# Queries and state of a recurrent attention moved into 64-row halves by DMA; x kept in w_in's row order; no state after the last group

## The chip, the cores and the metric

The kernel runs on 1 core of one Trainium2 chip. The metric is the device time of one launch in microseconds (us). Three runs of the kernel before took 397.42, 398.54 and 398.75 us; their median is 398.54 us.

## What is computed

Two blocks are joined. The first is a gated linear recurrence with a state per head, the second a feed-forward layer with a SoLU activation and a layer norm. The reference, cut to what matters:

```python
# q, k, v, alpha: (B=4, H=8, S=768, D=48)
state = np.zeros((B, H, D, D))
for t in range(S):
    state = alpha[:, :, t, :, None] * state + np.einsum('bhd,bhe->bhde', k[:, :, t], v[:, :, t])
    y[:, :, t] = np.einsum('bhd,bhde->bhe', q[:, :, t], state)
x = y.transpose(0, 2, 1, 3).reshape(B * S, H * D)      # 3072 x 384
h = x @ w_in                                           # 384 x 1024
e = np.exp(h - h.max(-1, keepdims=True))
solu = h * e / (e.sum(-1, keepdims=True) + 1e-09)
ln = (solu - mean(solu)) / np.sqrt(var(solu) + 1e-06) * g_ln
out = ln @ w_out                                       # 1024 x 384
```

The weights w_in and w_out arrive as 64-bit floats; the kernel reads both 32-bit words and makes f32 values of them.

## The kernel before, in words

The function that runs is `fast_path`. The 768 time steps are cut into 6 groups (G) of 128 (P). A group holds all 4 batches and all 8 heads, so 512 tokens (T4). Within a group the recurrence is turned into matrix products: scores of queries against keys under a triangular mask, the product of the masked scores with the values, and a read of the state that came in from the groups before. `scan_back` and `scan_on` are DVE scans that make the running products of alpha.

*Layout of a head.* A head has 48 rows (D). They are split into its first 32 (E0) and its last 16 (E1). Partitions hold four quarters of 32, one per batch. Blocks 0 to 7 hold the first 32 rows of the heads, blocks 8 to 11 the last 16 rows of two heads each. So `qv` has 16 blocks: 8 of first rows, and 8 in which the last rows of one head stand and those of its neighbour are zero (`apart` at L237 makes them from `qe` with `parity`). The state has the same 16 blocks, and `vn` holds the values with 80 columns (VW) per head, the last 16 dimensions at column 48.

*State read.* `read_state(n)` for n = 0 to 3 gives PE 32 matmuls each, through `y_mm` (L300): a tile of 32 rows by 32 columns at row 32b (batch) and column 32r. `read_values` adds the product of `vn` with the masked scores `sT` to the same PSUM banks (64 matmuls of 128 rows by 32 columns), and ACT copies them out as x (L331). `keys_back` (L287, L289) turns the keys round again, and `next_state` (L342, L349, L351) multiplies them with the values and adds to the state: 48 matmuls into two banks. `decay` (L251, L254) multiplies the state on POOL by the product of a whole group's alphas.

*Order of x.* The rows of x stand in blocks of 32 first dimensions of the heads, and then the last 16 of pairs of heads. To fit, `fetch` brings w_in's rows in this order: 16 copies of 32 or 16 rows for each call (L542).

*Feed-forward.* `up_mm` (L366) and `up_act` (L380 to L382) make h, e and the products; `down` (L477) multiplies with w_out, and `finish` (L495 to L511) scales and stores. `bits` (L572 to L584) makes f32 weights of the 64-bit ones on DVE, and `in_range` (L559, L560) tests their range on ACT.

*What sets the order.* It is written out by hand (`manual_schedule`); every engine works through its instructions in the order in which the program lists them. A first stretch handles group 0 and group 1's preparation. Then comes the loop over g = 1 to 5 with 8 steps s each. A step issues `up(g, s)`, half a `down` of the group before, and pieces of the attention of group g+1, which a table places in front (`head`), behind, in the middle or at the tail of the step:

```python
head={4: "keys_back", 5: "masked0", 6: "masked1"},
behind={0: "v keys", 1: "on2 on0 on1", 2: "lasts firsts", 3: "apart", 5: "decay", 6: "alpha", 7: "back"},
tail={4: "scores0", 5: "scores1", 6: "begin read0 read1", 7: "values"},
middle={7: "read2 read3"},
```

`masked` (L279) multiplies scores with the mask on DVE, `queries` (L244) and `keys` (L233) multiply with the alpha products on POOL, `firsts` and `lasts` (L184, L187) are DVE transposes. SP issues nearly all DMAs, in program order: loads of alpha, q, k (L132, L144), of v (L170; for group 0 L178, followed by POOL copies at L180), of weights (L542), and the stores (L511). In the compiled program each of these DMAs also waits for the eighth before it.

Of the kernel before, what the change touches and what calls it, by code (L numbers as in the profile page):

```python
# [9 lines left out]
FP = mybir.dt.float32  # L10
# [22 lines left out]
def fast_path(ctx, tc, q, k, v, alpha, moe_w_in, moe_w_out, moe_g_ln, out):  # L33
# [31 lines left out]
    const = pool("const", 1)  # L65
    two = pool("two", 4)
    ring = pool("ring", 3)
# [37 lines left out]

    VW = 80
    vn = const.tile([P, B, H, VW], FP, name="vn")
    state = const.tile([P, 2 * H, VW], FP, name="state")
    last = [slice(48, 80), slice(32, 64)]
    SW = P + 1  # L110
# [10 lines left out]
    kT = const.tile([P, NB, P], FP, name="kT")  # L121
    kg = const.tile([P, NB, P], FP, name="kg")
    sT = const.tile([P, B, H, P], FP, name="sT")
# [25 lines left out]
    def ends_of(src, tag=None):  # L149

        ends = ring.tile([P, T4], FP, name=tag) if tag else two.tile([P, T4], FP, tag="two", name="ends")
        ends = ends.rearrange("p (b d) -> p b d", b=B)
        nc.scalar.copy(out=ends.rearrange("p b (h d) -> p b h d", h=H), in_=by_token(src)[:, :, :, E0:D])
        return ends

    def turned(src, ends, out, blocks=range(NB)):

        x = by_token(src)
        for j in blocks:
            for b in range(B):  # L160
# [4 lines left out]
                )  # L165

    def load_v(g):
        t = slice(g * P, (g + 1) * P)
        for dst, src in ((slice(0, E0), slice(0, E0)), (slice(48, 64), slice(E0, D))):
            nc.sync.dma_start(  # L170
                out=vn[:, :, :, dst].rearrange("p b h d -> p (b h) d"),
                in_=v[:, :, t, src].rearrange("b h p d -> p (b h) d"),
            )

    def load_v_first(slot):
        x = slots[slot].rearrange("p (n d) -> p n d", d=D)
        y = vn.rearrange("p b h d -> p (b h) d")
        nc.sync.dma_start(out=x, in_=v[:, :, 0:P].rearrange("b h p d -> p (b h) d"))  # L178
        for dst, src in ((slice(0, E0), slice(0, E0)), (slice(48, 64), slice(E0, D))):
            nc.gpsimd.tensor_copy(out=y[:, :, dst], in_=x[:, :, src])  # L180


# [48 lines left out]
    def keys(g):  # L231
        for part in (slice(0, H), slice(H, NB)):
            nc.gpsimd.tensor_tensor(out=kT[:, part], in0=kT[:, part], in1=hk[:, part], op=ALU.mult)  # L233

    def apart():
        for i in range(2):
            nc.scalar.mul(  # L237
                out=qv[:, H : 2 * H].rearrange("p (j i) t -> p j i t", i=2)[:, :, i], in_=qe, mul=parity[:, i : i + 1]
            )
# [6 lines left out]
    def decay(g):  # L246

        if g == 0:
            return
        s = state[:, 0:H, 0:64]  # L250
        nc.gpsimd.tensor_tensor(out=s, in0=s, in1=h4[:, 0:H, 1:2].to_broadcast([P, H, 64]), op=ALU.mult)  # L251
        for i in range(2):
            s = state[:, H : 2 * H, 0:64].rearrange("p (j i) e -> p j i e", i=2)[:, :, i]
            nc.gpsimd.tensor_tensor(out=s, in0=s, in1=h4[:, H:NB, 1:2].to_broadcast([P, NP, 64]), op=ALU.mult)  # L254

# [28 lines left out]
    def keys_back(g, t=None):  # L284
        t = t or banks("tp", [NP, P], 3)
        for j in range(NB):
            nc.tensor.transpose(out=t[j // NP][:, j % NP], in_=kT[:, j], identity=ident)  # L287
        for i in range(3):
            nc.scalar.copy(out=kg[:, NP * i : NP * i + NP], in_=t[i])  # L289

    parts = [(a, [(NP * a + r, slice(0, E0)) for r in range(NP)]) for a in range(2)]
    parts += [(2, [(2 * r + i, last[i]) for r in range(NP)]) for i in range(2)]
    reading = {}

    def y_mm(b, a, r, row, lhsT, rhs, stop=False):
        begun = reading["begun"]
        nc.tensor.matmul(  # L300
            y_bank(b)[quarter(r), a], lhsT=lhsT, rhs=rhs, start=(b, r) not in begun, stop=stop,
            tile_position=(row, 32 * r), skip_group_check=True,
        )
        begun.add((b, r))
# [9 lines left out]

    def read_state(n):
        a, hs = parts[n]
        for rows in (0, H):
            for r, (h, e) in enumerate(hs):
                for b in range(B):
                    p = quarter(b)  # L320
                    y_mm(b, a, r, 32 * b, state[p, rows + h, e], qv[p, rows + h])

    def read_values(g, batches=range(B)):
        if 0 in batches:
            gr[g]["x"] = pair.tile([P, KC, B, P], FP, name="x")
        for b in batches:
            for n, (a, hs) in enumerate(parts):
                for r, (h, e) in enumerate(hs):
                    y_mm(b, a, r, 0, vn[:, b, h, e], sT[:, b, h], n == len(parts) - 1)
        for b in batches:  # L330
            nc.scalar.copy(out=gr[g]["x"][:, :, b], in_=reading["y"][b])  # L331

    def next_state(g):
        kv = banks("kv", [H, 64], 2)
        for j in range(NB):
            for b in range(B):
                if j < H:
                    o, e = kv[0][quarter(b), j], vn[:, b, j, 0:64]
                else:
                    i = 2 * (j - H)  # L340
                    o, e = kv[1][quarter(b), i : i + 2], vn[:, b, i : i + 2, 0:64]
                nc.tensor.matmul(  # L342
                    o, lhsT=kg[:, j, quarter(b)], rhs=e, start=True, stop=True, tile_position=(0, 32 * b),
                    skip_group_check=True,
                )
        for i in range(2):
            s = state[:, H * i : H * i + H, 0:64]
            if g == 0:
                nc.scalar.copy(out=s, in_=kv[i])  # L349
            else:  # L350
                nc.vector.tensor_tensor(out=s, in0=s, in1=kv[i], op=ALU.add)  # L351

# [30 lines left out]
    def running(g, f):  # L385

        d = gr[g]
        if f == 1:
            d["p"] = one.tile([P, 2, T4], FP, name="p")
            if g == G - 1:  # L390
                d["pu"] = two.tile([P, T4], FP, tag="two", name="pu")
        if g == G - 1:
# [54 lines left out]
    def last_norm():  # L447
# [4 lines left out]
        for b in range(B):  # L452
            for r in range(4):
# [4 lines left out]
                )  # L458
        tt = two.tile([P, B, 32], FP, tag="two", name="cols_u")
        nc.vector.transpose(out=tt.rearrange("p b t -> p (b t)"), in_=t.rearrange("p b t -> p (b t)"))  # L460
# [68 lines left out]
    def fetch(i, slot, n=1):  # L529
# [6 lines left out]
        else:  # L536
            rows = moe_w_in[:, f * P : f * P + w].rearrange("(h d) f -> h d f", d=D)
            parts = [(slice(E0 * r, E0 * r + E0), c, rows[NP * c + r, 0:E0]) for c in range(2) for r in range(NP)]
            parts += [(slice(E1 * h, E1 * h + E1), 2, rows[h, E0:D]) for h in range(H)]
        for rows, c, src in parts:  # L540
# [21 lines left out]
    def bits(i, part=None):  # L562
# [3 lines left out]
        if part != 1:  # L566
            made[i] = [
                two.tile([P, F], FP, tag="two", name=x).rearrange("p (c f) -> p c f", c=hi.shape[1])
                for x in ("top", "low")
            ]  # L570
# [66 lines left out]
    nc.gpsimd.memset(state, 0.0)  # L637
    load_v_first(0)
    fetch(0, 3, 2)
# [12 lines left out]
    t = three("tp_a", [(ps_a, "a0"), (ps_a, "a1"), (ps_a, "a2")])  # L652
    turned(an, ends_of(an), t)
    for i in range(3):
        nc.scalar.copy(out=aT[:, NP * i : NP * i + NP, 1:SW], in_=t[i])  # L655
        scan_back(0, i)
    t = three("tp_k", [(ps_a, "a3"), (ps_h, "h"), (ps_h, "h")])
    turned(kn, ends_of(kn), t)
    alpha_over(0)
# [5 lines left out]
    t = three("tp_q", [(ps_o, "o"), (ps_o, "o"), (ps_a, "a0")])  # L665
    turned(qn, ends_of(qn), t)
    for i in (2, 0, 1):
# [82 lines left out]
    nc.vector.tensor_tensor(out=qe, in0=tq[2], in1=aT[:, H:NB, 1:SW], op=ALU.mult)  # L750
    apart()
    finish(0)
    decay(1)
    in_range(7)
    for i in range(2):
        scan_on(1, i)
        part = slice(NP * i, NP * i + NP)
        nc.vector.tensor_tensor(out=qv[:, part], in0=tq[i], in1=aT[:, part, 1:SW], op=ALU.mult)  # L758
    down(2, 0)
    scores(1, 0)  # L760
# [10 lines left out]
    read_begin()  # L771
    read_state(0)
    read_state(1)
    down(3, 1)
    read_state(2)
    read_state(3)
    alpha_over(2)
    load(alpha, an, 3)
    for i in range(3):
# [3 lines left out]
    load(k, kn, 3)  # L783
    scan_on(2, 2)
    scan_on(2, 0)
    read_values(1)
# [7 lines left out]
        behind={0: "v keys", 1: "on2 on0 on1", 2: "lasts firsts", 3: "apart", 5: "decay", 6: "alpha", 7: "back"},  # L794
        tail={4: "scores0", 5: "scores1", 6: "begin read0 read1", 7: "values"},
        middle={7: "read2 read3"},
    )
    first = dict(
        head={3: "keys_back", 5: "masked0", 6: "masked1"},
        behind={0: "v", 1: "on1", 2: "lasts firsts", 3: "apart", 5: "decay", 7: "alpha back"},  # L800
        tail={4: "scores0", 5: "scores1", 6: "begin read0 read1", 7: "values"},
        middle={7: "read2 read3"},
    )

    def attend(a, what):
# [9 lines left out]
        elif what[:2] == "on":  # L815
            scan_on(a, int(what[2]))
        elif what == "lasts":
            lasts(qn, qe)
# [7 lines left out]
        elif what == "apart":  # L826
            apart()
        elif what == "decay":
            decay(a)
        elif what == "keys_back":  # L830
            keys_back(a)
        elif what[:6] == "scores":
# [15 lines left out]
        elif what == "values":  # L848
            read_values(a)
            next_state(a)  # L850

# [530 lines left out]
```

## Time and profile before

| | |
|---|---|
| span of the profiled execution | 399.0 us |
| time of the runs, median (range) | 398.54 us (397.42 to 398.75) |
| PE busy | 378.3 us, 95%, 4929 records |
| weight loads (PEld) busy | 229.1 us, 57% |
| DVE / ACT / POOL busy | 254.3 / 145.9 / 115.6 us |
| up and down projections on PE (L366, L477) | 135.5 and 133.6 us |
| state read (L300, qv and state) | 1280 records, mean 278 ns |
| next state (L342) | 576 records |
| keys back (L287) | 72 records |
| mean granted PE clock | 0.985 |

How to read it: PE is the matmul engine, PEld its weight loads, which run beside it. A group of instructions is named by line, engine, operation and `out<-in`, with the tile's shape (rows*columns) for PE. A 32-bit matmul leaves two records. Many small matmuls run at once on different parts of the array, so the busy times of single records overlap, and the cost of a stage is read from the timeline: the start of what follows minus its own start. In the timeline a row is the start in us, the length in us, engine, line, operation, and the number of records merged; brackets hold the idle time before it and what ended it. A window's row names the busy time of every engine, the granted clock, the share of the DMA engines and GB/s.

### The profile page before, as it was taken

To read this page: it belongs to the slowest core of one execution; us is meant where nothing else is said; L and a number is where in the kernel's file an instruction comes from. 1 tells how busy PE (TensorE), PEld (TensorE's weight loads), DVE (VectorE), ACT (ScalarE), POOL (GpSimd) and SP (SyncE) were. 2 spreads that over 40 slices of the span, in tenths; PEclk is the share of its full clock that TensorE was granted. 3 is DMA by queue.
4 is the path that set the end of the run, shared out by engine and by line. 5 is a ranking of instruction groups with operands and counts; after the bars stand their busy time and mean duration, and the time that the engine had idled before them with its cause. 6 is when DMAs were issued, how large, how long until landed. Compare 5 with 4: busy or idle time off the path is not lost. (4 is left out here: it accounts for less than half of the span.)

```text
span 399.0 us, 11125 instructions
## 1 busy us (share of the span) xinstructions
PE 378.3 (95%) x4929; PEld 229.1 (57%) x4929; DVE 254.3 (64%) x415; ACT 145.9 (37%) x253; POOL 115.6 (29%) x118
## 2 busy tenths in 40 slices
PE   8686999987989999999999999999999999999995
PEld 8673435555665457555557555666556575555552
DVE  1977878996897858795574884665864413444510
ACT  2634657644314415224253143342152132223200
POOL 5010000021031993438130456210475110333200
PEclk9996999998999999999999999999999999999999
DMA  9967958511366302913040931004200000000011
GB/s 184 196 165 174 224 185 160 134 28 60 81 161 99 81 3 65 161 45 92 2 102 26 155 89 32 14 11 74 28 20 21 23 3 21 20 21 18 24 41 48
DMA packets 86409, 30.82 MB, mean 77 GB/s; under 512 B 67912, under 2 KB 84560, under 8 KB 86352
## 3 DMA queue, kind: packets, MB, share of 16 engines
q1 hardware_dynamic: 85328, 29.11, 34.0%
q8 instruction: 40, 0.66, 0.7%
q10 hardware_dynamic: 1024, 0.92, 0.7%
q14 instruction: 17, 0.14, 0.1%
HBM read 25.30 MB, written 4.72 MB: 75 GB/s over the span
## 5 line engine op out<-in xcount | busy, mean ns | idle before, releaser
L366 PE MATMUL h<-x,w_in 128*128 128x512 f32 x288 | 135.5, 610 | 4.1 <-ACT sq L559 3.6
L477 PE MATMUL o<-w_out,room 128*128 128x385 f32 x384 | 133.6, 492 | 1.1 <-DVE least L223 1.1
L477 PEld LDWEIGHTS o<-w_out,room 128*128 128x128 f32 x384 | 71.8, 191 | 57.3 <-issue 16.3
L366 PEld LDWEIGHTS h<-x,w_in 128*128 128x128 f32 x288 | 53.2, 192 | 64.2 <-issue 50.7
L381 DVE TENSOR_TENSOR room<-h,e 128x512 f32<-128x512 f32 x40 | 27.5, 688 | 61.7 <-ACT e L380 61.7
L508 POOL TENSOR_TENSOR r<-sums,mhalf 128x1 f32<-128x1 f32 x20 | 12.1, 607 | 169.2 <-DVE sums L500 169.2
L380 ACT ACTIVATE e<-h 128x512 f32<-128x512 f32 x40 | 23.8, 596 | 91.9 <-PE h L366 91.9
L397 POOL TENSOR_TENSOR p<-p,e 128x512 f32<-128x512 f32 x30 | 40.9, 1365 | 24.7 <-ACT e L380 24.4
L382 ACT ACTIVATE u<-room 128x512 f32<-128x512 f32 x40 | 25.2, 631 | 42.2 <-DVE room L381 42.2
L279 DVE TENSOR_TENSOR sT<-a,mask 128x512 f32<-128x512 f32 x44 | 27.3, 683 | 16.1 <-PE a L268 16.1
L268 PE MATMUL a<-qv,kT 32*128 32x128 f32 x704 | 26.0, 286 | 4.7 <-DVE qv L758 2.0
L397 DVE TENSOR_TENSOR p<-p,u 128x512 f32<-128x512 f32 x30 | 24.7, 822 | 8.7 <-ACT u L382 8.7
L268 PEld LDWEIGHTS a<-qv,kT 32*128 32x128 f32 x704 | 22.9, 193 | 11.9 <-issue 3.3
L209 DVE TENSOR_TENSOR_SCAN hT<-aT,unit 128x516 f32<-128x516 f32 x18 | 22.2, 1282 | 8.2 <-ACT aT L655 8.1
L209 DVE TENSOR_TENSOR_SCAN aT<-aT,seed 128x516 f32<-128x516 f32 x18 | 25.7, 1428 | 0.6
L300 PE MATMUL y<-sT,vn 128*32 128x128 f32 x768 | 22.8, 274 | 1.4 <-issue 0.9
L300 PEld LDWEIGHTS y<-sT,vn 128*32 128x32 f32 x768 | 20.8, 110 | 4.0 <-issue 2.5
L233 POOL TENSOR_TENSOR kT<-kT,hT 128x1024 f32<-128x1024 f32 (+1 forms) x8 | 13.3, 1685 | 30.9 <-DVE kT L184 30.9
L331 ACT COPY x<-y 128x384 f32<-128x384 f32 x24 | 11.2, 480 | 26.4 <-PE y L300 26.4
L300 PEld LDWEIGHTS y<-qv,state 32*32 32x32 f32 x1280 | 15.3, 103 | 7.6 <-issue 4.1
L300 PE MATMUL y<-qv,state 32*32 32x128 f32 x1280 | 19.0, 278 | 0.0
L201 ACT ACTIVATE sq<-an,mone 128x1536 uint8<-128x1536 f32 x12 | 18.8, 1571 | 0.2
(140 smaller groups left out, 372.7 us busy)
## 6 DMA issues: line engine op xcount, KB each, us to landing
an<-in_alpha_dram SPq DMA_DIRECT2D x20, 192.0 KB, 4.1
out_dram<-o_sb SPq DMA_DIRECT2D x20, 192.0 KB, 1.9
room<-in_moe_w_out_dram SPq DMA_DIRECT2D x8, 384.0 KB, 3.9
kn<-in_k_dram SPq DMA_DIRECT2D x16, 192.0 KB, 3.9
qn<-in_q_dram SPq DMA_DIRECT2D x16, 192.0 KB, 3.5
vn<-in_v_dram SPq DMA_DIRECT2D x5, 512.0 KB, 5.4
room<-in_moe_w_in_dram SPq DMA_DIRECT2D x16, 128.0 KB, 3.8
kn<-in_k_dram SPq DMA_DIRECT2D x4, 384.0 KB, 5.7
```

Of the source, the lines that this page charges most:

```text
L201: nc.scalar.activation(out=sq, in_=x, func=AF.Relu, scale=sign, bias=mone, accum_out=over[:, g, i : i + 1])
L209: nc.vector.tensor_tensor_scan(out=o, data0=a, data1=s, initial=1.0, op0=ALU.mult, op1=ALU.add)
L233: nc.gpsimd.tensor_tensor(out=kT[:, part], in0=kT[:, part], in1=hk[:, part], op=ALU.mult)
L268: nc.tensor.matmul(a[b][:, i], lhsT=kT[quarter(b), kb], rhs=qv[quarter(b), qb], start=kb == h, stop=kb != h, tile_position=(32 * b, 0), sk ...
L279: nc.vector.tensor_tensor(out=sT[:, b, half * NP : half * NP + NP], in0=a[b], in1=mask[:, None, :].to_broadcast([P, NP, P]), op=ALU.mult,)
L300: nc.tensor.matmul(y_bank(b)[quarter(r), a], lhsT=lhsT, rhs=rhs, start=(b, r) not in begun, stop=stop, tile_position=(row, 32 * r), skip_g ...
L366: nc.tensor.matmul(h, lhsT=w_in[:, a, f * P : (f + 1) * P], rhs=d["x"][:, a].rearrange("p b t -> p (b t)"), start=(a == 0), stop=(a == KC ...
L380: nc.scalar.activation(out=e, in_=h, func=AF.Exp)
L381: nc.vector.tensor_tensor(out=u, in0=h, in1=e, op=ALU.mult)
L382: nc.scalar.activation(out=u2, in_=u, func=AF.Square)
L397: eng.tensor_tensor(out=p, in0=d[0][i] if f == 1 else p, in1=d[f][i], op=ALU.add)
L477: nc.tensor.matmul(d["o"][:, 0 : DM + 1], lhsT=u_of(g, f)[:, b * P : b * P + P], rhs=w_out[:, f], start=(f == 0), stop=(f == FC - 1), skip ...
```

## The change

It has three parts that go together. First, the state, the values and the keys turned round get 64 columns per head, 48 of them used, and the state stands in two halves of 64 partitions, 48 used: batch b is in half b // 2, in column block b % 2. The queries are made as before, in quarters of 32 rows; `move_q` then copies them by DMA into `q64` in the new layout, 12 copies a group: per batch the first rows of all heads, and two copies of last rows. `move_decay` does the same for the decays. A state read is then one matmul of 48 rows per head and output block where there were two of 32 rows. Second, x stands in w_in's own row order: an output block of 32 columns that crosses two heads is made by two matmuls into the same place (`last`), with zeros beside the values. `fetch` brings w_in in copies of 128 rows. Third, the last group no longer turns its keys round and makes no state. The pool `two` is replaced by four fixed slots in `lot`, three of which `q64` takes over later; v comes in one copy per batch, for group 0 too, without POOL copies.

```diff
-    VW = 80
-    vn = const.tile([P, B, H, VW], FP, name="vn")
-    state = const.tile([P, 2 * H, VW], FP, name="state")
-    last = [slice(48, 80), slice(32, 64)]
+    HW = 64
+    VW = H * HW + E1
+    vn = const.tile([P, B, VW], FP, name="vn")
+    state = const.tile([P, 2, VW], FP, name="state")
+    lot = const.tile([P, 4 * 768], FP, name="lot")
+    lots = [lot[:, 768 * i : 768 * i + 768] for i in range(4)]
+    q64 = lot[:, 0 : 2 * H * P].rearrange("p (c h t) -> p c h t", c=2, h=H)
+    dec64 = const.tile([P, 2, H], FP, name="dec64")
...
-    kg = const.tile([P, NB, P], FP, name="kg")
+    kg = const.tile([P, B, H, HW], FP, name="kg")
...
+    def held(x, n):
+        return x[:, n, 0 : H * HW].rearrange("p (h e) -> p h e", e=HW)[:, :, E1:HW]
...
-        for dst, src in ((slice(0, E0), slice(0, E0)), (slice(48, 64), slice(E0, D))):
-            nc.sync.dma_start(
-                out=vn[:, :, :, dst].rearrange("p b h d -> p (b h) d"),
-                in_=v[:, :, t, src].rearrange("b h p d -> p (b h) d"),
-            )
+        for b in range(B):
+            nc.sync.dma_start(out=held(vn, b), in_=v[b, :, t, :].rearrange("h p d -> p h d"))
...
+    def moved(dst, firsts_, lasts_):
+        for b in range(B):
+            i, c = divmod(b, 2)
+            lo = 64 * i
+            nc.sync.dma_start(out=dst[lo : lo + E0, c], in_=firsts_[32 * b : 32 * b + 32])
+            to = dst[lo + E0 : lo + D, c].rearrange("d (j k) t -> d k j t", k=2)
+            for k in range(2):
+                at = 32 * b + E1 * k
+                nc.sync.dma_start(out=to[:, k], in_=lasts_[at : at + E1])
+    def move_q():
+        moved(q64, qv[:, 0:H], qe)
+    def move_decay(g):
+        moved(dec64[:, :, :, None], fend[:, g, 0:H, None], fend[:, g, H:NB, None])
...
-        s = state[:, 0:H, 0:64]
-        nc.gpsimd.tensor_tensor(out=s, in0=s, in1=h4[:, 0:H, 1:2].to_broadcast([P, H, 64]), op=ALU.mult)
-        for i in range(2):
-            s = state[:, H : 2 * H, 0:64].rearrange("p (j i) e -> p j i e", i=2)[:, :, i]
-            nc.gpsimd.tensor_tensor(out=s, in0=s, in1=h4[:, H:NB, 1:2].to_broadcast([P, NP, 64]), op=ALU.mult)
+        for c in range(2):
+            x = held(state, c)
+            nc.gpsimd.tensor_tensor(
+                out=x, in0=x, in1=dec64[:, c, :, None].to_broadcast([P, H, D]), op=ALU.mult
+            )
...
-        for i in range(3):
-            nc.scalar.copy(out=kg[:, NP * i : NP * i + NP], in_=t[i])
-    parts = [(a, [(NP * a + r, slice(0, E0)) for r in range(NP)]) for a in range(2)]
-    parts += [(2, [(2 * r + i, last[i]) for r in range(NP)]) for i in range(2)]
+        for i in range(2):
+            nc.scalar.copy(
+                out=kg[:, :, NP * i : NP * i + NP, 0:E0].rearrange("p b j d -> p j b d"),
+                in_=t[i].rearrange("p j (b d) -> p j b d", b=B),
+            )
+        for m in range(2):
+            nc.scalar.copy(
+                out=kg[:, :, m::2, E0:D].rearrange("p b j d -> p j b d"),
+                in_=t[2].rearrange("p j (b k d) -> p j b k d", b=B, k=2)[:, :, :, m],
+            )
+    def first(h):
+        return slice(HW * h + E1, HW * h + D) if h % 2 == 0 else slice(HW * h + E0, HW * h + HW)
+    def last(h):
+        return slice(HW * h + D, HW * h + D + E0) if h % 2 == 0 else slice(HW * h, HW * h + E0)
+    parts = []
+    for j in range(NP):
+        parts += [(3 * j, 2 * j, first), (3 * j + 1, 2 * j, last), (3 * j + 2, 2 * j + 1, first)]
+    parts += [(3 * j + 1, 2 * j + 1, last) for j in range(NP)]
...
-    def read_state(n):
-        a, hs = parts[n]
-        for rows in (0, H):
-            for r, (h, e) in enumerate(hs):
-                for b in range(B):
-                    p = quarter(b)
-                    y_mm(b, a, r, 32 * b, state[p, rows + h, e], qv[p, rows + h])
+    def read_state(half):
+        for n, h, e in parts[8 * half : 8 * half + 8]:
+            for c in range(2):
+                for i in range(2):
+                    p = slice(64 * i, 64 * i + D)
+                    y_mm(2 * i + c, n, 64 * i, state[p, c, e(h)], q64[p, c, h])
...
-        kv = banks("kv", [H, 64], 2)
-        for j in range(NB):
-            for b in range(B):
...
+        kv = banks("kv", [H, D], 2)
+        for h in range(H):
+            for c in range(2):
+                for i in range(2):
+                    b = 2 * i + c
+                    nc.tensor.matmul(
+                        kv[c][64 * i : 64 * i + 64, h], lhsT=kg[:, b, h],
+                        rhs=vn[:, b, HW * h + E1 : HW * h + HW], start=True, stop=True,
+                        tile_position=(0, 64 * i), skip_group_check=True,
+                    )
...
-            rows = moe_w_in[:, f * P : f * P + w].rearrange("(h d) f -> h d f", d=D)
-            parts = [(slice(E0 * r, E0 * r + E0), c, rows[NP * c + r, 0:E0]) for c in range(2) for r in range(NP)]
-            parts += [(slice(E1 * h, E1 * h + E1), 2, rows[h, E0:D]) for h in range(H)]
+            parts = [(slice(0, P), c, moe_w_in[c * P : (c + 1) * P, f * P : f * P + w]) for c in range(KC)]
...
+    nc.gpsimd.memset(kg, 0.0)
+    nc.gpsimd.memset(dec64, 0.0)
-    load_v_first(0)
+    load_v(0)
...
     apart()
+    move_decay(1)
     finish(0)
     decay(1)
...
+    move_q()
     down(2, 0)
     scores(1, 0)
...
     read_state(0)
+    down(3, 1)
     read_state(1)
-    down(3, 1)
-    read_state(2)
-    read_state(3)
...
-        tail={4: "scores0", 5: "scores1", 6: "begin read0 read1", 7: "values"},
-        middle={7: "read2 read3"},
+        tail={4: "scores0", 5: "scores1", 6: "begin read0", 7: "values"},
+        middle={7: "read1"},
...
             scan_on(a, int(what[2]))
+            if what == "on2":
+                move_decay(a)
...
             apart()
+            move_q()
...
         elif what == "keys_back":
-            keys_back(a)
+            if more:
+                keys_back(a)
...
             read_values(a)
-            next_state(a)
+            if more:
+                next_state(a)
```

## The prediction on record

> **What bounds the kernel now.** I read the page's busy shares first, then the table by stage (stages cut at my own times), then the timeline of one group, then the waits. The table by stage gives, for each window, its length, then busy time and instruction records of PE, PEld, DVE, ACT and POOL, the granted clock, the DMA share and GB/s:
>
> ```profile
> 26.00:62.00 36.00, 31.93 (x245) 14.90 (x236) 26.55 (x35) 21.44 (x43) 0.00 (x0) 0.91 0.75 179
> 62.00:93.00 31.00, 27.10 (x317) 15.95 (x320) 29.55 (x46) 17.08 (x34) 3.66 (x4) 1.00 0.52 108
> 93.00:118.00 25.00, 23.23 (x630) 17.63 (x630) 19.69 (x29) 9.60 (x14) 4.51 (x5) 0.93 0.42 107
> 166.00:220.00 54.00, 54.00 (x757) 32.84 (x756) 35.03 (x59) 19.94 (x33) 19.57 (x20) 1.00 0.27 64
> 274.00:328.00 54.00, 54.00 (x683) 32.19 (x685) 29.29 (x50) 16.25 (x28) 20.62 (x19) 1.00 0.16 31
> ```
>
> From about 118 us PE never stops, and DVE, ACT and POOL stand idle a third of the time or more: there a microsecond of PE work is a microsecond of the span. From 26 to 93 us DVE is the fuller engine (29.55 of 31 us in the second window), so what starts DVE earlier counts there. The chain of waits holds only the last 0.8 us, so it does not help. The PE timeline of group 3's attention (groups count from 0; start, length, records; the next start minus this start is what a stage costs):
>
> ```profile
> 178.77 1.47 PE L287 MATMUL tp<-ident,kT 128*128 128x128 f32 x12
> ...
> 180.08 2.74 PE L366 MATMUL h<-x,w_in 128*128 128x512 f32 x6
> ...
> 200.07 1.90 PE L300 MATMUL y<-qv,state 32*32 32x128 f32 x128
> ...
> 201.90 2.84 PE L366 MATMUL h<-x,w_in 128*128 128x512 f32 x6
> ...
> 204.67 1.90 PE L300 MATMUL y<-qv,state 32*32 32x128 f32 x128
> ...
> 206.50 2.86 PE L477 MATMUL o<-w_out,room 128*128 128x385 f32 x8
> 209.29 3.70 PE L300 MATMUL y<-sT,vn 128*32 128x128 f32 x128
> ...
> 212.81 1.95 PE L342 MATMUL kv<-vn,kg 128*32 128x64 f32 x96
> ...
> 214.69 2.84 PE L366 MATMUL h<-x,w_in 128*128 128x512 f32 x6
> ```
>
> So in one group: keys back 180.08-178.77 = 1.31 us; the state read 1.83+1.83 = 3.66; values 3.52; next state 1.88. At the start, the waits for the first weights and the SP issues of w_in (min/median/max ns):
>
> ```profile
> DVE top L572 <- DMA room<-in_moe_w_in_dram: 2.3, 1, 2.3
> PE h L366 <- ACT sq L559: 3.6, 1, 3.6
> L542 SPq DMA_DIRECT2D room<-in_moe_w_in_dram x32: 418/419/4762, 12.7 to 33.9; - x32
> 33.19 5.46 PE L366 MATMUL h<-x,w_in 128*128 128x512 f32 x6 [3.65 <-ACT sq L559]
> ```
>
> DVE, free at 26.2, waits until 28.51 for w_in; PE then idles 3.65 us, and its first up projection takes 5.46 us for what later takes 2.84: the clock was halved (0.61 in the window 36 to 40).
>
> **What the Trainium skill says.** "TensorEngine Tiling (Array Packing)", section Tiling Modes: 32x32 gives 16 independent tiles, 64x32 gives 8. The trace agrees for four tiles: 128 records of values in 3.52 us are 27.5 ns each, a quarter of the 109 ns (1.31/12) that a record costs on the whole array. But the state read on 16 tiles takes 1.83/128 = 14.3 ns per record, not 109/16 = 6.8: it is bound by the number of records, not by tiles. "TensorE: Matmul & The Clock Gate", Part 3, says matmuls start and end in strict program order. If so, two neighbours on one tile would hold up the queue. An f32 matmul is two records on one tile, next to each other in the compiled program, yet the trace of the first scores shows the second passes behind the first passes of other tiles:
>
> ```profile
> 21.45 0.38 PE L268 MATMUL a_h<-qv,kT 32*128 32x128 f32 x2 [0.19 <-DVE qv L671]
> 21.47 0.38 PE L268 MATMUL a_o<-qv,kT 32*128 32x128 f32 x2
> 21.67 0.28 PE L268 MATMUL a_h<-qv,kT 32*128 32x128 f32 x2
> ```
>
> So one tile's queue does not stop the others, at least one record deep. The same page, LDWEIGHTS, prices a load at its columns / 1.2 ns; here 32 columns take 110 ns and 128 take 191, 0.84 ns per column, which agrees. "DMA: Bandwidth & Descriptors", Rules for kernel authors: small transfers pay mostly overhead; here a 1 KB transfer landed in 3.5 us, a 192 KB one in 1.9 to 4.1.
>
> **The change part by part**, against the 399.0 us of the profiled span.
>
> (1) State read, five groups. 64 matmuls (128 records) per half become 32 (64 records), on 8 tiles instead of 16. By records: 64 x 14.3 = 0.92 us. By tiles: 64 x 109/8 = 0.87. I add 0.2 for the drain that does not shrink: 1.1 per half against 1.83, saves 0.73, times 10 halves = 7.3 us. The program now puts two matmuls of one tile (four records) near each other before it moves to the next column of tiles; no row shows that deep a queue. Bounds: if it blocks, four tiles work at a time, 64 x 109/4 = 1.74 per half, which saves 0.9 in all; at best exactly half, 9.2. All of it lies in PE's dense part.
>
> (2) No state of the last group: keys back 1.31 and next state 1.88 go from PE (3.2 us), with ACT's copies and DVE's adds, which were hidden. 3.2 us.
>
> (3) Next state, five groups: 48 matmuls (96 records, 32 columns of weights, 4 tiles) become 32 (64 records, 64 columns, 2 tiles). A load of 64 columns is 53 ns by the skill's price, the 48-column matmul shorter; hidden behind each other as in values: 64/2 x 53 = 1.7 us against 1.88. If loads did not hide, 64/2 x (53+45) = 3.1. I take 1.85: nothing; ends -1 and +6 us, the upper unlikely since in values the loads (110 ns) fit within 110 ns per tile.
>
> (4) w_in: 32 copies of 16 or 32 rows become 6 of 128. In the compiled program each copy waits for the eighth before it, and each costs 0.42 us of SP, so the first 16 (12.7 to 25.7 us) land by 28.5. Now the first three are issued right after v, by about 19 us. Their 1.57 MB at the 244 GB/s that 18 to 21 us moved take 6.4 us: about 25, before DVE is free at 26.2. DVE's 2.3 us wait goes, and what is late next is DVE itself (26.55 of 36 us, with bits and the products in turn). PE's idle falls from 3.65 to about 1.3 us; if then the clock is not halved, DVE's 1.76 us wait for the first exp goes as well. 2.3 + half of 1.76 = 3.1 us; ends 0 (another wait takes it) and 4.1.
>
> (5) move_q, new: 12 copies per group on SP, SBUF to SBUF, 768 KB. In group 3 the last query product on POOL ends at 178.09+2.63 = 180.7. 12 x 0.42 us of issue plus up to 0.5 for the eighth-before rule end at 186.3, landing 1.9 to 3.9 later: 190. The read starts at 200.07: cover 10 us. Behind it on SP stands the out copy of 185.9, half a microsecond late; ACT's next write to that buffer is two finishes away. In group 1 the product ends at 92.81, landing by 100.2 to 102.2, the read at 104.04: cover 2 to 4 us, with scores and down between. Less if these run at full clock (3.08 against 2.07): cost 0, upper end 1 us. The alpha load behind it (97.83) moves by up to 1 us, landing at about 104.3, before its transpose at 104.72.
>
> (6) move_decay: 12 tiny copies per group, 5 us of SP plus 3.5 to land. Usual groups: from 168 to 177, needed at 186.65, cover 10 us; the q load behind it starts at 178. Group 1: from 84.0 to about 93, so decay on POOL ends near 94.4 instead of 90.6 (two of 384 elements instead of 512 and 2 x 256). Behind it on POOL stands r of the second finish (93.35), 1 us later, then o_sb and the alpha check on ACT: the same alpha load, at worst 1 us on DVE, none on PE.
>
> (7) v in runs of 192 bytes instead of 128 and 64; its POOL copies at 20.28 go; one more memset on POOL before 8 us; four copies for kg on ACT instead of three (+0.3 us, under PE's dense run). Values keep 64 matmuls. Nothing.
>
> Sum: 7.3 + 3.2 + 0 + 3.1 = 13.6. 399.0 - 13.6 = 385.4 for the profiled execution; the median of the runs (398.54) is 0.5 below its span, so 384.9.
>
> **The rivals.** (a) *Tiles block*: strict order holds, the state read saves 0.9: 398.54 - (0.9+3.2+3.1) = 391.3. For it: the skill's sentence; against it: the first scores. Chance 0.18. (b) *The early start is lost*: by 62 us DVE or a w_out load is as late as before: 398.54 - 10.5 = 388.0. For it: DVE idles 9.4 of 36 us there for several releasers. Chance 0.12. (c) *Slower: the queries land late.* One place: the first read of each group behind the 12 copies of move_q. Cover from last product to read is 19.4 us in usual groups and 11.2 in group 1; with w the wait in a usual group, the gain is gone when 4w + (w+8.2) = 13.6, w = 1.1, that is when a copy takes SP about 1.45 us instead of 0.42. At 1.7 us (q's first loads, of many short runs, took 1.7 and 2.9): 12 x 1.7 + 3 = 23.4, w = 4.0, in all 28 us: 398.5 - 13.6 + 28.2 = 413. Against it: rows here are 2 to 4 KB, like w_in's at 0.42. Chance 0.05.
>
> **How the numbers follow.** Forecast 384.9 (its own range 381 to 388) 0.62, (a) 0.18, (b) 0.12, (c) 0.05, within 0.3% by a mixture 0.03. Faster by over 0.3% (1.2 us, about what a measurement of this kernel can tell from no change): 0.62+0.18+0.12 = 0.92; same 0.03; slower 0.05. Range: best ends 9.2+3.2+1+4.1 = 17.5, 381.0; up to rival (a) and a bit of loss in group 1, 392.3. Left out: (c), the mixture.
>
> **What would show it.** Right: y from state with 64 records per half, next start about 1.1 us on; no keys back or next state in the last group; DVE's first bits near 26.2 us with no DMA wait; PE waiting nowhere for the copies to the 64-row halves. Wrong: state-read halves near 1.8 us (a); the start of the loop still near 118 us minus only the state read's share (b); PE idle before the first read with a DMA as releaser (c).

## The result and the profile after

The changed kernel takes 396.95 us (median of 20 runs, 396.31 to 398.55); the kernel before, beside it, 398.73 us (20 runs, 397.4 to 401.72). The ratio is 0.9956, with a 95% interval from 0.9938 to 0.9975: faster by 0.44%, or 1.8 us, where 13.6 us were forecast. The profiled execution has a span of 395.8 us, 3.2 less than before's 399.0. PE is busy for 370.0 us in 4021 records (before 378.3 us in 4929).

Most of what was forecast for single stages can be seen. The timeline of PE for group 3's attention, after:

```profile
201.51 1.44 PE L330 MATMUL y<-lot,state 48*32 48x128 f32 x64
202.88 2.84 PE L390 MATMUL h<-x,w_in 128*128 128x512 f32 x6
...
213.45 2.07 PE L367 MATMUL kv<-vn,kg 128*64 128x48 f32 x64
215.45 1.98 PE L390 MATMUL h<-x,w_in 128*128 128x512 f32 x4
```

Half a state read now costs 202.88 - 201.51 = 1.37 us (before 1.83, forecast 1.1), next state 2.00 us (before 1.88). In the last group there is no keys back and no next state. At the start, PE's timeline shows the first up projection, and the scores of group 1 (62 of their 64 records):

```profile
31.02 2.79 PE L390 MATMUL h<-x,w_in 128*128 128x512 f32 x6
...
89.00 2.06 PE L281 MATMUL a<-qv,kT 32*128 32x128 f32 x62 [1.23 <-DVE qv L782]
```

Before, the first up projection stood at 33.19 (5.46 us long), and the scores at 92.87:

```profile
92.87 3.08 PE L268 MATMUL a<-qv,kT 32*128 32x128 f32 x62 [2.02 <-DVE qv L758]
```

So 3.9 us were won by here, and DVE's wait for w_in is gone (its first weights are begun at 26.31). But from here to the end of the span the changed kernel takes 395.8 - 89.0 = 306.8 us, and the kernel before took 399.0 - 92.87 = 306.1. Of what the state read and the last group should save, 10.5 us by forecast, nothing is left there: as much was lost somewhere. The table by stage, after (window, length, busy time and records of PE, PEld, DVE, ACT, POOL, granted clock, DMA share, GB/s), says where:

```profile
26.00:62.00 36.00, 33.27 (x343) 17.94 (x345) 29.21 (x39) 23.89 (x49) 0.00 (x0) 1.00 0.65 175
...
89.00:128.50 39.50, 31.87 (x488) 20.45 (x489) 26.92 (x42) 12.17 (x19) 7.21 (x9) 0.91 0.49 113
...
166.00:220.00 54.00, 54.00 (x598) 32.58 (x597) 34.92 (x56) 19.73 (x34) 20.37 (x19) 1.00 0.33 77
```

In the second row PE stands idle for 7.6 of 39.5 us and the clock falls to 0.91. PE's timeline there, after:

```profile
98.57 2.25 PE L330 MATMUL y<-lot,state 48*32 48x128 f32 x64
...
104.91 3.70 PE L330 MATMUL y<-sT,vn 128*32 128x128 f32 x128
...
111.51 5.42 PE L390 MATMUL h<-x,w_in 128*128 128x512 f32 x12
123.84 4.83 PE L390 MATMUL h<-x,w_in 128*128 128x512 f32 x6 [6.92 <-DVE room L405]
128.51 1.47 PE L300 MATMUL tp<-ident,kT 128*128 128x128 f32 x12
```

The same stretch of the kernel before:

```profile
118.19 7.99 PE L366 MATMUL h<-x,w_in 128*128 128x512 f32 x18
126.02 1.47 PE L287 MATMUL tp<-ident,kT 128*128 128x128 f32 x12
```

The loop's first up projection starts 6.7 us earlier than before (111.51 against 118.19). Then the third one waits 6.92 us for the first activation's product (room, L405) and runs at half clock (4.83 us for what takes 2.84). At group 2's keys back the changed kernel is 2.5 us late (128.51 against 126.02). From the first scores to this place it takes 39.5 us instead of 33.15: 6.4 us lost. From there to the end it takes 267.3 instead of 273.0: 5.7 us won. 3.9 - 6.4 + 5.7 = 3.2.

Who made DVE late stands in DVE's timeline, after:

```profile
105.47 2.19 DVE L180 STREAM_TRANSPOSE aT<-an 128x1024 f32<-128x1024 f32 x1 [6.13 <-DMA an<-in_alpha_dram]
...
123.09 0.69 DVE L405 TENSOR_TENSOR room<-h,e 128x512 f32<-128x512 f32 x1 [1.27 <-ACT e L404]
```

DVE, done with its work for group 1 at 99.3, waits 6.13 us for alpha of group 2. Then it works for 17.6 us through group 2's preparation (transposes, scans, the state's additions) before it comes to the product. In the kernel before the same chain began at 104.72 with no wait, and its product stood at 122.49:

```profile
104.72 2.07 DVE L184 STREAM_TRANSPOSE aT<-an 128x1024 f32<-128x1024 f32 x1
...
122.49 0.69 DVE L381 TENSOR_TENSOR room<-h,e 128x512 f32<-128x512 f32 x1 [1.27 <-ACT e L380]
```

SP's timeline, after, shows what stood in front of that load:

```profile
89.58 0.55 SPq L236 DMA_DIRECT2D lot<-qv  x1
...
97.06 1.24 SPq L240 DMA_DIRECT2D lot<-qe  x2
98.40 0.53 SPq L535 DMA_DIRECT2D out_dram<-o_sb  x1
99.02 1.91 SPq L135 DMA_DIRECT2D an<-in_alpha_dram  x4
```

The queries' 12 copies fill SP from 89.58 to 98.3, behind the decay's 12, which fill it from 81.11 to 88.8. One issue costs 0.6 us, where 0.42 was counted. The decay's copies did not hold up the queries' here, as the last query product ends only at 88.95.

The queue is not the whole of DVE's wait. The load must also wait for ACT's pass over the alpha that it overwrites. ACT's timeline has the end of this pass in the changed kernel, SP's the load in the kernel before:

```profile
95.39 0.19 ACT L197 ACTIVATION_READ_ACCUMULATOR sq<-an,mone 128x1 f32 x1
97.83 1.82 SPq L132 DMA_DIRECT2D an<-in_alpha_dram  x4
```

Before, the load went out as soon as the pass ended (97.80). After, the pass ended at 95.58, only 2.2 us earlier than before, while DVE was free 5.4 us earlier. The copies on SP then added 3.4 us (95.58 to 99.02). The pass itself was held up too: the decay on GpSimd waited for its copies, and r of the second finish, whose sums were ready at 89.4, ran behind it at 91.11, 1.7 us late; ACT had waited for this r. So an estimate from these figures splits the 6.13 us into 3.4 of queue, 1.7 by way of the decay, and 1.0 that would be left with no copy in the way. No run takes these parts one by one.

### The profile page after: what moved, and what is told of

It reads as the page before. It is cut to its first block, busy times and chain, and to the rows that moved or that the text cites. A ratio compares the mean times of both kernels' runs of the same rounds, so it can differ in the third digit from the quotient of the medians.

```text
span 395.8 us, 9496 instructions
## 1 busy us (share of the span) xinstructions
PE 370.0 (93%) x4021; PEld 222.1 (56%) x4021; DVE 252.2 (64%) x413; ACT 144.4 (36%) x255; POOL 111.6 (28%) x113
## 5 line engine op out<-in xcount | busy, mean ns | idle before, releaser
L405 DVE TENSOR_TENSOR room<-h,e 128x512 f32<-128x512 f32 x40 | 27.6, 690 | 63.6 <-ACT e L404 63.6
L281 PE MATMUL a<-qv,kT 32*128 32x128 f32 x704 | 24.8, 278 | 3.3 <-DVE least L219 1.8
L281 PEld LDWEIGHTS a<-qv,kT 32*128 32x128 f32 x704 | 22.0, 186 | 10.1 <-POOL p L421 2.2
L330 PEld LDWEIGHTS y<-lot,state 48*32 48x32 f32 x640 | 12.1, 106 | 6.9 <-issue 5.1
L534 ACT ACTIVATE o_sb<-o,r 128x384 f32<-128x384 f32 x16 | 9.3, 584 | 17.1 <-POOL r L532 17.1
```

The source lines that it names most:

```text
L281: nc.tensor.matmul(a[b][:, i], lhsT=kT[quarter(b), kb], rhs=qv[quarter(b), qb], start=kb == h, stop=kb != h, tile_position=(32 * b, 0), sk ...
L330: nc.tensor.matmul(y_bank(b)[quarter(r), a], lhsT=lhsT, rhs=rhs, start=(b, r) not in begun, stop=stop, tile_position=(row, 32 * r), skip_g ...
L405: nc.vector.tensor_tensor(out=u, in0=h, in1=e, op=ALU.mult)
```

## The experiments

Theory A: alpha's load of group 2 stands behind the copies on SP; it lands too late for DVE, and this takes back what the reads have won. Rival B: DVE's own chain sets the time of that product, whenever alpha comes. A second question was why half a read takes 1.37 us and not 1.1.

| kernel | median us | first scores of group 1 at | from there to the end of the span |
|---|---|---|---|
| before | 398.7 | 92.87 | 306.1 |
| changed | 396.95 | 89.00 | 306.8 |
| early alpha | 392.68 | 88.09 | 301.7 |
| queries' copies on GpSimd | 400.05 | 88.01 | 309.0 |
| w_in in more copies | 399.03 | 90.11 | 306.7 |
| last group's state made | 399.94 | 87.78 | 309.7 |
| before, with early alpha | 400.23 | 90.84 | 306.4 |
| early alpha, decay's copies on GpSimd | 390.02 | 87.87 | 300.3 |
| read in another order | 394.7 | 89.40 | 305.3 |
| last rows of the queries first | 390.98 | 89.35 | 300.15 |
| early alpha, decay on GpSimd, other order | 389.23 | 89.42 | 298.5 |
| the same, one scan later | 388.65 | 87.89 | 298.8 |

The two right columns are of one profiled execution each. The start differs between executions of kernels that do not differ there (87.78 to 89.42 in nine of them), so the last column compares better what lies behind it. The medians come from four sets of runs, in which the kernel before had 398.73, 398.66, 399.03 and 399.73 us. Each ratio below is to the kernel before of the same set; the changed kernel's is 0.9956.

### Early alpha

```diff
+    alpha_over(1)
     load(q, qn, 2)
+    load(alpha, an, 2)
...
     finish(1)
-    alpha_over(1)
-    load(alpha, an, 2)
```

> Group 2's alpha load (and the ACT check that must come before it) is put ahead of the 24 copies of group 1 on SP, right behind group 2's q load. Theory A (the alpha load is late because it stands behind move_q on SP, and this takes back what the start and the state read had gained by 105 us): DVE's wait of 6.1 us for alpha goes, PE's wait of 6.9 us at the third up projection of group 1 falls to about 1, its clock is not halved: 389 to 392 us against 397; part may come back as a wait of the first state read, since the copies of q64 go out some 2.6 us later. Rival B (DVE's own chain from the alpha transpose to the first product of group 1, 17.6 us, sets this point whatever alpha does): within 1 us of 397.

392.68 us (391.57 to 394.6, 4 runs), ratio 0.9863 [0.9795, 0.9931]. DVE's timeline:

```profile
98.33 2.00 DVE L180 STREAM_TRANSPOSE aT<-an 128x1024 f32<-128x1024 f32 x1
```

No wait stands behind it any more, and PE waits 1.5 us in all for the products (changed kernel 9.1). B falls. The time is 0.7 us outside A's range, and PE's waits name the reason, which the expectation had named as possible:

```profile
PE y L330 <- DMA lot<-qe: 2.4, 2, 1.4
```

The load now stands in front of the 24 copies; the queries' are issued from 91.37 to 100.0, and the first read, at 97.65, has to wait for them. The wait has moved to the next transfer on the same queue. The edit moves the load out of the queue and ACT's pass forward at once, so it shows that the lateness of the load is the cause, and not which of the two made it late.

### The queries' copies on GpSimd's queue

Only group 1's 12 copies of the queries are issued from GpSimd.

```diff
-    move_q()
+    move_q(nc.gpsimd)
```

> Only group 1's move_q is issued from POOL's queue instead of SP's; the alpha load keeps its place. Theory A: SP is free at 89 us, the alpha load goes out at about 95.6, when ACT's check ends, and not at 99.0; it lands 3.4 us earlier, DVE's wait falls from 6.1 to about 2.7, and the time to 392 to 394 us. Rival B: 397. If POOL's copies come later than SP's did, the first state read waits and eats it.

400.05 us (398.09 to 401.71, 20 runs), ratio 1.0031 [1.0008, 1.0055]. A's number is missed by 6 us or more, on the wrong side. GpSimd's timeline:

```profile
96.09 1.02 POOL L240 DMA_DIRECT2D lot<-qe  x2
97.13 0.57 POOL L532 TENSOR_TENSOR r<-sums,mhalf 128x1 f32<-128x1 f32 x1
```

GpSimd computes as well, and does so in order. Its 12 issues (90.10 to 97.1) hold up r of the second finish. ACT's output copy waits for r, and ACT's pass over alpha stands behind that copy; the load may overwrite alpha only when the pass is done. It was issued at 101.63 instead of 99.02, and DVE waited 9.04 us instead of 6.13. The read itself was on time (2.00 us, no wait for a DMA). So the step is the same, alpha's load, made late by another route, and the edit was a bad test of SP's queue.

### w_in in more copies

15 copies a fetch, of 32 or 16 rows, in place of 3 of 128 rows.

```diff
-            parts = [(slice(0, P), c, moe_w_in[c * P : (c + 1) * P, f * P : f * P + w]) for c in range(KC)]
+            cuts = [(0, 32), (32, 64), (64, 96), (96, 112), (112, 128)]
+            parts = [
+                (slice(lo, hi), c, moe_w_in[c * P + lo : c * P + hi, f * P : f * P + w])
+                for c in range(KC) for lo, hi in cuts
+            ]
```

> w_in comes in 15 copies of 16 or 32 rows for each fetch, as many as before the change, in place of 3; all else as in the changed kernel. My step on the start: DVE's first weights at 28.5 us again instead of 26.2, the first scores of group 1 about 3.9 us later, and since the alpha load follows these on SP, the end too: 400 to 401 us. Rival (what the start gains is lost at 105 us anyway): 397.

399.03 us (397.21 to 401.63, 20 runs), ratio 1.0008 [0.9986, 1.0031]. That is 2.1 us over the changed kernel, and 1 us short of what was expected. DVE's wait for w_in is back, 1.28 us long (before 2.3), and its first weights are begun at 27.76. The first up projection starts at 32.43 and takes 4.47 us, the scores stand at 90.11, and the rest is as long as in the changed kernel (306.7). So step (4) is real, and it passes through to the end. By the medians the number of copies makes about half of the 3.9 us; the one profile puts the scores only 0.7 to 2.3 us behind those of the nine kernels with three copies. What makes the other half was not tried.

### The last group's state made again

```diff
         elif what == "keys_back":
-            if more:
-                keys_back(a)
+            keys_back(a)
...
             read_values(a)
-            if more:
-                next_state(a)
+            next_state(a)
```

> The last group turns its keys round and makes its state again, as before the change. My step: PE is dense there, so 1.3 us of keys back and 2.0 of next state come back: 400.2 us. Rival (other engines set the last groups): 397.

399.94 us (399.06 to 401.3, 20 runs), ratio 1.0033 [1.001, 1.0056]: 3.0 us over the changed kernel, 2.9 in the last column. Step (2) is as forecast.

### The kernel before, with early alpha

The same move as in the first experiment, in the kernel before. Its start is its own.

> The kernel before, with only alpha's load of group 2 (and ACT's pass over alpha that it waits for) moved ahead of the queries' multiplication of group 1, as in the early-alpha version of the changed kernel. Theory A (the load is late only because the two sets of 12 copies stand in front of it on SP, and because everything else has moved forward): in the kernel before the load landed before its transpose at 104.72 us and nothing waited, so the time stays at 398.0 to 399.5 us. Rival C (an early alpha is a gain of its own, whatever the copies): 393 to 395 us.

400.23 us (396.5 to 401.12, 14 runs), ratio 1.0002 [0.9969, 1.0035]. The median lies above the range of A, but the kernel before had 399.03 in the same set of runs. An early alpha is worth nothing to the kernel before (last column 306.4 against 306.1), and C falls: the 4 to 5 us that it brings the changed kernel are a loss undone, not a gain of its own.

### Early alpha, and the decay's copies on GpSimd

In group 1 GpSimd issues the decay's copies, behind the r of the first finish.

```diff
-    move_decay(1)
     finish(0)
+    move_decay(1, nc.gpsimd)
     decay(1)
```

> The changed kernel with the early alpha load, and in group 1 the 12 copies of the decay issued from GpSimd's queue, behind the first finish, so that the 12 copies of the queries are no longer behind 24 issues on SP. Theory A (what was left of the loss with the early load alone, 392.7 us, is the read of the state waiting 2.4 us for the last queries, because SP issues 24 copies one after the other at 0.6 us each): queries land some 4 us sooner, the wait goes, 389 to 391 us. Rival D (the read is then held by the state's decay, whose copies are no quicker on the other queue, or by the second finish behind them on GpSimd): 392 to 395 us.

390.02 us (389.32 to 391.57, 6 runs), ratio 0.9773 [0.9726, 0.9821]. The last query is issued by 96.4 (100.0 with early alpha alone), and PE no longer waits for a DMA in the read. It fits theory A; D falls. From the first scores to the end it takes 300.3 us, 6.5 less than the changed kernel. PE's timeline shows what is left at the third up projection:

```profile
116.50 4.54 PE L390 MATMUL h<-x,w_in 128*128 128x512 f32 x6 [2.48 <-DVE room L405]
```

### The read in another order

```diff
-        for n, h, e in parts[8 * half : 8 * half + 8]:
-            for c in range(2):
+        for c in range(2):
+            for n, h, e in parts[8 * half : 8 * half + 8]:
                 for i in range(2):
```

> The changed kernel, with the 32 matmuls of a half of the state's read in another order: all of c = 0 first and then all of c = 1, so that a tile of TensorE is used again only after seven others and not after one. Nothing else differs. Theory E (the half takes 1.37 us instead of 1.1 because two neighbours on one tile hold each other up): a half falls to 1.1 to 1.2 us, and the time by 8 x 0.2 = 1.6 us or more, to 394.5 to 395.5 us. Rival F (what sets the half is the rate at which records of this size come over eight tiles, whatever their order): a half stays at 1.37 us and the time at 397 us.

394.7 us (394.5 to 396.52, 6 runs), ratio 0.9889 [0.9842, 0.9935]. PE's timeline in group 3:

```profile
202.12 1.16 PE L330 MATMUL y<-lot,state 48*32 48x128 f32 x64
203.21 2.84 PE L390 MATMUL h<-x,w_in 128*128 128x512 f32 x6
```

A half costs 1.09 us, with the same matmuls on the same tiles, now with five to nine others between two on one tile: F falls, and the order is the cause. That it is the tile that holds up its neighbour, as theory E says, is argued: the order also changes which PSUM banks are written one after the other (two batches in turn instead of four), and no run parts the two. Of the 8 x 0.28 = 2.2 us in groups 2 to 5, 1.5 show in the last column. In group 1, DVE still waits 6.03 us for alpha, and what the reads win there goes into that wait.

### The last rows of the queries first

As the version with the decay on GpSimd, and the eight copies of the queries' last rows are issued as soon as `qe` is ready.

```diff
     apart()
+    move_q((1,))
...
-    move_q()
+    move_q((0,))
```

> As the version with the early alpha load and the decay's copies on GpSimd's queue, and in group 1 the eight copies of the queries' last columns are issued as soon as these are ready (some 6 us before the first columns), so that only four copies are left to issue when the first columns are ready. Theory A: the last query of group 1 lands 4 to 5 us sooner again; if the read was still waiting for it, it no longer does: 388.5 to 390.5 us; if the version before had no such wait left, no difference to it, within 0.7 us. Rival D (the decay or the second finish holds the read): the same time as the version before, 392 to 395 us.

390.98 us (389.24 to 391.33, 6 runs), ratio 0.9777 [0.973, 0.9823]. It is 1 us over the version before it by the medians, a little more than the 0.7 allowed for, but with intervals that overlap almost wholly, and the rest after the scores is the same (300.15 against 300.3). The read had no wait left; D falls again.

### Both

The decay on GpSimd, early alpha, and the other order of the read.

> The early alpha load with the decay's copies on GpSimd's queue, and the other order of the state's read, together. Theory (the two losses are of different places: one in the preparation of group 2, one in the reads of groups 2 to 5): they add. From 390.0 us, eight halves at 1.1 us instead of 1.37 save 2.2 us, and two more in group 1 if its reads no longer wait: 387 to 388.3 us. Rival (the reads' gain is taken back by the next wait of DVE's chain): 389.5 to 390.5 us.

389.23 us (388.85 to 389.7, 6 runs), ratio 0.9737 [0.9694, 0.9779]. From the scores to the end the order saves 300.3 - 298.5 = 1.8 us. The medians say 0.8; this version's profile shows a start 1.5 us later, which may be the difference. The losses add within what the starts leave uncertain; the time itself came out 1 us over the theory's range and just below the rival's, so by the time alone this is not decided.

### One scan later

```diff
     scan_on(2, 2)
     move_decay(2)
-    scan_on(2, 0)
...
-        behind={0: "v", 1: "on1", 2: "lasts firsts", 3: "apart", 5: "decay", 7: "alpha back"},
+        behind={0: "v", 1: "on0 on1", 2: "lasts firsts", 3: "apart", 5: "decay", 7: "alpha back"},
```

> As the version with both, and the second of group 2's three forward scans moved behind the second activation of group 1 in the loop, out of DVE's chain between alpha's transpose and the first product of the feed-forward part (1.56 us of DVE by the trace). Theory (what is left of TensorE's wait for that product, 2.5 us at the third up projection of group 1, ends with DVE's chain): the wait falls to about 1 us, and the clock that follows a wait recovers: 385 to 387 us. Rival (the wait moves to the next link, the fourth up projection or the queries of group 2): the same time as the version with both.

388.65 us (387.61 to 390.07, 6 runs), ratio 0.9727 [0.9682, 0.9771]: not told apart from the version with both. The wait for the product fell from 2.77 to 1.35 us, but PE's waits have a new line:

```profile
PE a L281 <- POOL qv L257: 1.7, 1, 1.7
```

The scan that was put off makes the queries of group 2 late, as the rival said, and the granted clock falls after this wait, to 0.54 from 127.8 to 130.0: the up projection at 129.87 takes 3.58 us instead of 2.84. From the first scores to the end it takes 298.8 us against 298.5.

## Why the prediction was wrong

The direction was right, and so were most of the stages. The time was missed because of one step, and three terms had another size.

| step | forecast, us | measured, us |
|---|---|---|
| (1) state read | saves 7.3 | saves 0.46 a half, 3.7 in the eight halves of groups 2 to 5 |
| (2) last group | saves 3.2 | saves 3.0 |
| (3) next state | 0 | costs 0.12 each, with new waits of 0.6 to 0.8 for x around it |
| (4) start | saves 3.1 | saves 3.9 in the two profiled executions |
| (5), (6) the copies and alpha's load | 0 on PE | most of the 6.4 lost by group 2's keys back |

*The step that failed* is the end of (5) and of (6): "The alpha load behind it (97.83) moves by up to 1 us, landing at about 104.3, before its transpose at 104.72", and "the same alpha load, at worst 1 us on DVE, none on PE". The load was found, and so was the queue in front of it, but its cover was counted wrongly. First, the due time of 104.72 belongs to the kernel before. In the changed kernel DVE is free for the transpose at 99.3: the start is 3.9 us earlier, and the first scores and the projection behind them, at full clock, take 1.6 us less. The load could not follow, as ACT's pass and the copies stood before it. Second, 12 copies of the queries cost 12 x 0.64 = 7.7 us and not 12 x 0.42 = 5.0 (with gaps, 8.7 in the profile). By the estimate above DVE would wait 2.7 us even with no queue on SP: 1.7 by way of the decay's copies, which (6) had put at 1, and 1.0 by the due time alone.

Third, PE waited as well: DVE's chain is 17.6 us long and ends at the product for which the third up projection waits. The kernel before shows the same chain, from 104.72 to 122.49, with PE right behind it. It was not followed, because there was no idle time in it. That the late load is the cause is shown: moved forward, it takes 5.1 us out of the changed kernel (306.8 to 301.7) and nothing out of the kernel before. With the decay's copies off SP too, 6.5 us are back.

Rival (c) was a transfer that comes late behind the queries' copies on SP. It had the mechanism, but it named the wrong transfer, the queries themselves, in every group. In the loop they were never late. In group 1 the first read takes 2.18 us (98.57 to 100.75), and 1.38 where the queries are issued earlier (97.43 to 98.81 in the version with the decay on GpSimd), so some 0.8 us of late queries is likely there, though the profile names no wait; in the changed kernel it stands behind the wait for alpha.

*Step (1)* left a term open: how deep a queue one tile may have before its neighbours on the array have to wait. The forecast took 0.2 us of drain and no blocking, 1.1 us; complete blocking would give 1.74. With two matmuls for the same tile near each other in the program a half takes 1.37 us, and with five to nine other matmuls between two on one tile 1.09 us. So the forecast's size was that of an order of the loops that the change does not have. That it fits that order to 0.01 us is in part luck: nothing measured the 0.2 us of drain. The Trainium skill, "TensorE: Matmul & The Clock Gate", Part 3, says that matmuls start and end in strict program order. The other order's gain fits it, if a matmul whose tile is busy holds up those behind it, though not as much as complete blocking would. This is a reading and not shown: what share is the tile's, the queue's or the PSUM banks' was not tried.

*Step (3)*: the shape with 64 columns takes 2.00 us against 1.88, inside the range given. The 53 ns used there are not the length of such a load: in the trace a load of 64 columns lasts 138 ns, where 32 columns take 110 and 128 about 190, so only the difference per column agrees with the price. PE now comes to next state before ACT has copied x: after group 2's values PE waits 0.76 us for x, and in the last group, where no next state stands in between, 0.60. (1), (2) and (3) together then explain 5.1 of the 5.7 us won behind group 2's keys back: 8 x 0.46 + 3.2 - 0.6 for the last group - 0.9 in group 2 - 0.24 in groups 3 and 4 = 5.1. The other 0.6 is unexplained.

*Step (4)* is right in its mechanism; its size differs between executions. The first scores of the kernel before stand at 92.87 and, in its version with early alpha, at 90.84; those of nine kernels with w_in in three copies a fetch at 87.78 to 89.42. The gain is 1.4 to 5.1 us by these. The halved clock of the first up projection, 5.46 us in the profile of the kernel before, is not always there either: in its version with early alpha, which does not differ at the start, that projection took 2.81.

With the early alpha load and the decay's copies off SP the changed kernel takes 390.0 us, inside the whole range given (381.0 to 392.3) but not in the forecast's own (381 to 388); with the read's order too, 389.2. Against 384.9 there then remain 4.3 us, for which (3) and its waits, the 2.8 us wait that is left at the third up projection, and the varying start can be named; they were not taken apart one by one.

## What to carry to other kernels

When a change moves work forward, count the cover of each transfer against the times at which its reader will be ready afterwards; a load that does not move with the rest becomes the new limit, even if it had no wait before. Copies put on a queue push back everything behind them, and moving them to another queue can push back other work (GpSimd's own products here), so first move forward the loads that depend on nothing new, together with the work that they wait for. Try an order of small matmuls in which the other tiles come before one tile is used again.

## What the runs showed of the hardware

- A copy from SBUF to SBUF of 16 or 32 rows costs SP 0.60 us of issue (0.64 from one to the next), where w_in's copies of 16 or 32 rows from HBM cost 0.42. On GpSimd one issue took 0.5 to 0.7 us, in which it computed nothing.
- 64 records of 48 rows on eight tiles took 1.37 us (21.4 ns each) or 1.09 us (17.0 ns each), by their order alone.
- The clock could fall after waits of 1.7 to 2.8 us. The Trainium skill, "TensorE: Matmul & The Clock Gate", Part 1, names an idle window of about 3.4 us. Here a wait of 6.92 us was followed by a projection of 4.83 us, and waits of 2.48 and 2.77 us by 4.54 and 4.51 us, where the full clock takes 2.84. In the kernel before, 62 records of the scores took 3.08 us after a wait of 2.02, and 2.06 after 1.23 in the changed kernel; with one scan later, a wait of 1.71 us was followed by a granted clock of 0.54. After 1.35 us, and after 1.66 in the kernel before with early alpha, the projection took its full-clock time (2.84 and 2.81). As 1.66 and 1.71 us went different ways, the length of the wait alone does not decide it there; what does was not tried.
